# A fixed instruction order per period for an attention-and-mixer kernel: merged TensorE visits, a tail product inside another tile, and a last output tile in columns

## The chip, the cores and the metric

The kernel runs on one core of a Trainium2 chip. The metric is the device time of one execution in microseconds (us). A profile is one execution recorded by the hardware profiler; it gives every instruction of every engine with its start time. The engines are PE (TensorE, matrix products, with PEld for its weight loads), DVE (VectorE), ACT (ScalarE), POOL (GpSimd) and SP (SyncE, which here only issues transfers). PSUM is the small memory into which PE writes; SBUF is the large one from which all engines read.

## The reference, cut to what matters

Eight batches, each a Longformer attention followed by an MLP-Mixer block. Sequence 576, eight heads of 64, so a row of the block's input has 512 numbers.

```python
# attention, per batch and head; window 32, 8 global positions
mask   = (abs(i - j) <= 32) | is_global[i] | is_global[j]
attn   = softmax(where(mask, q @ k.T / 8, -1e9))
x      = concat_heads(attn @ v)                       # [576, 512]
# mixer, per batch
h      = relu(x.T @ w_tok1) @ w_tok2                  # token products: 576 -> 256 -> 576
u      = x + h.T
out    = u + relu(u @ w_ch1) @ w_ch2                  # channel products: 512 -> 1536 -> 512
```

576 rows are four tiles of 128 and one tail of 64. The tail has a path of its own in several places below.

## The kernel before: the parts that the change touches

The kernel works in periods. In period b the *dense* part is the channel products of batch b, and the *sparse* part, dealt out between the dense units, is attention and token products of batch b+1 and the scores of batch b+2. Every engine executes its instructions in the order in which they are written. Names of the steps as the text uses them:

- `T` transposes Q and K of two heads on PE, `TR` the last 64 rows; `TE`, `TRE` copy the results from PSUM to SBUF on DVE.
- `S_` the banded scores of two heads, in two parts, on PE in an arrangement of four 64x64 tiles; `SX` their exponential on ACT; `SM` the masks on DVE, first the 8 global columns (`eg`), then the band.
- `GK`, `OG` the global rows, on PE in 128x32 tiles; `LX`, `LM` and `RF` what ACT and DVE do with them.
- `PV` attention times V for one row tile, on PE in 128x64 tiles; then reciprocal and multiplication on DVE into `x16s`.
- `M1`, `M2` the two token products, 128x128; `M3` transposes u with DMA; `M4` the first channel product (4 matmuls of 512 columns and a ReLU on ACT), `M4l` the same for the tails of two batches; `M5` the second channel product (half a row tile: 6 matmuls of 512 columns).

```python
def S_(b, p, part):
    ps = pss([P, 2, 512], name=f"s{part}_{b}_{p}")          # one of two PSUM buffers, in turn
    for j in js:
        for par in range(2):
            nc.tensor.matmul(ps[o, par, i0 - a : i1 - a], lhsT=kT[r, HQ * j : HQ * j + HQ], rhs=qf[r, i0:i1], ...)
    st[b]["s", p, part] = ps
    if b > 0:
        SX(b, p, part)
# ... cut ...
def PV(b, tau):
    sh = 64 if tau == NT - 1 and b % 2 == 1 else 0
    tiles = ((2 * tau, 0), (2 * tau + 1, 64)) if tau < NT - 1 else ((2 * tau, sh),)   # last tile: one half only
    ps = (pss if b != 2 and tau % 2 else psv)([P, 2, 512], name=f"pv_{b}_{tau}")
    for hf in range(2):
        glob(hf)                      # 264 columns for each tile
        for hh in range(NP):
            local(hf, hh)             # 66 columns for each tile and head
    # ... cut: reciprocal and multiplication on DVE into x16s[b % 2][:, tau] ...
def M2(b, part):
    taus = ((0, 1), (2, 3), (4,))[part]
    ps = pss([P, 2, 512], name=f"hp_{b}_{part}")
    for i, tau in enumerate(taus):
        for ch in range(2):
            nc.tensor.matmul(ps[:, i, :], lhsT=w2[:, ch, P * tau - sh : P * tau - sh + P], rhs=s["a1"][:, ch, :], ...)
    # ... cut: x + ps on DVE; part 2 is the tail of 64 rows, 128x512 of which 64 rows are used ...
def M5(b, tau, part):
    if part == 0:
        s["o"] = psm([P, 512], name=f"op_{b}_{tau}")
    for j in range(6 * part, 6 * part + 6):
        nc.tensor.matmul(ps, lhsT=w, rhs=wc2[:, j, :], start=(j == 0), stop=(j == NJ - 1))
    # ... cut: part 1 adds u on DVE and stores 128 rows of 512 ...
# ... cut: the loads and the head (batch 0), which is written out step by step; its end: ...
    M2(0, 2)
    masks_a()
    for p in (None, 0):
        cast_qk(1, 0, p, V)           # casts of batch 1's q and k on DVE, after their loads
        cast_qk(1, 1, p, V)
# period 0: D is the next dense unit; n = 1, m = 2
u = [D, D, D, D, D, D, lambda: TR(n), lambda: globals_(n), D, lambda: t(n, 0), *c1[:2], D]
# ... cut ...
# second half of a later period, m = b + 2
return [D, s2(m, 0), D, lambda: t(m, 3), lambda: SM(m, 0), D, s2(m, 1), D, lambda: SM(m, 1), D, s2(m, 2), D,
        lambda: SM(m, 2), lambda: GK(m), lambda: v_odd(m), s2(m, 3), D, lambda: SM(m, 3), D, lambda: OG(m)]
```

`s2(m, p)` is both parts of the scores of one pair of heads; a later period has four such visits, three of `PV` (two tiles, two tiles, the last tile) and one of `TR`.

Of the kernel before, what the change touches and what calls it, by code (L numbers as in the profile page):

```python
# [8 lines left out]
F32 = mybir.dt.float32  # L9
# [16 lines left out]

def merge(sparse, dense):


    ts, td = sum(c for c, _ in sparse) or 1.0, sum(c for c, _ in dense) or 1.0  # L30
    i = j = 0
    a = d = 0.0
    while i < len(sparse) or j < len(dense):
        if j >= len(dense) or (i < len(sparse) and a / ts <= d / td):
            a += sparse[i][0]
            sparse[i][1]()
            i += 1
        else:
            d += dense[j][0]
            dense[j][1]()  # L40
            j += 1
# [3 lines left out]
def kernel(  # L45
# [27 lines left out]
    psS = ctx.enter_context(tc.tile_pool(name="psS", bufs=2, space=bass.MemoryType.PSUM))  # L73
# [5 lines left out]
    def pss(shape, dtype=F32, name="s"):  # L79
        return psS.tile(shape, dtype, tag="s", name=name)  # L80
# [4 lines left out]
    def psm(shape, dtype=F32, name="m"):  # L85
        return psM.tile(shape, dtype, tag="m", name=name)

# [156 lines left out]
    w1l = const.tile([P, 2, DTOK], F16)  # L244
# [7 lines left out]
    def load_w1l():  # L252
        nc.gpsimd.dma_start(out=w1l[0:LAST, 0], in_=moe_w_tok1[S - LAST : S, :])
        nc.gpsimd.dma_start(out=w1l[LAST:P, 1], in_=moe_w_tok1[S - LAST : S, :])
# [40 lines left out]
    def x_pads(i):  # L295
        nc.gpsimd.memset(x16s[i][LAST - 64 * i : P - 64 * i, NT - 1, :], 0.0)

# [35 lines left out]
    def gather_t(t):  # L333
        pg = (psm if t == 0 else psv)([P, 2, P], F16, name=f"pg_{t}")
        for ti in range(2):
            if t > 0:
                nc.vector.tensor_copy(out=g16[ti][t], in_=g32[ti][t])
            nc.tensor.transpose(out=pg[:, ti, :], in_=g16[ti][t], identity=ident)
        st[0]["gt", t] = pg
        if t > 0:  # L340
            GTE(t)
            GKE(t)
# [53 lines left out]
    def T(b, p):  # L396
        pT = (psm if b in (0, 2) else psv if b == 1 or p % 2 else pss)([P, 2, 512], F16, name=f"pT_{b}_{p}")
# [23 lines left out]
    def TR(b):  # L421
        pr = (psm if b in (0, 2) else psv)([P, 2, 4, NP * 16], name=f"pr_{b}")
# [8 lines left out]
        if b > 0:  # L431
            TRE(b)
# [10 lines left out]
    def S_(b, p, part):  # L443
        qf = qTs[b % 2][:, p].rearrange("p t x -> p (t x)")
        kT = kTs[b % 2][:, p]
        ps = pss([P, 2, 512], name=f"s{part}_{b}_{p}")
# [16 lines left out]
        if b > 0:  # L463
            SX(b, p, part)
# [43 lines left out]
    def GK(b):  # L508
        s = st[b]
        ps = (psv if b != 2 else pss)([P, 2, 512], name=f"gk_{b}")  # L510
# [8 lines left out]
        if b > 0:  # L519
            LX(b)  # L520
            LM(b)
# [12 lines left out]
    def OG(b):  # L534
        s = st[b]
        ps = (psv if b != 2 else pss)([P, 2, VW], name=f"og_{b}")
        for c in range(NT):
# [5 lines left out]
        rf = mb.tile([P, NP, 2, VW], F16, tag="rf", name=f"rf_{b}")  # L543
        nc.vector.tensor_tensor(
            out=rf, in0=ps.unsqueeze(1).to_broadcast([P, NP, 2, VW]),
            in1=blk.rearrange("p (n r) -> p n r", r=2).unsqueeze(3).to_broadcast([P, NP, 2, VW]), op=ALU.mult,
        )
        s["rf"] = rf
# [52 lines left out]
    def M1_0(p):  # L601
# [8 lines left out]
        for tt in range(2):  # L610
            for ch in range(NT):
                w = w1[:, ch, P * tt : P * tt + P] if ch < NT - 1 else w1l[:, 0, P * tt : P * tt + P]
                nc.tensor.matmul(ps[:, tt], lhsT=w, rhs=x16s[0][:, ch, cols], start=(ch == 0), stop=(ch == NT - 1))
# [33 lines left out]
    def PV(b, tau):  # L647
        s = st[b]

        sh = 64 if tau == NT - 1 and b % 2 == 1 else 0  # L650
        tiles = ((2 * tau, 0), (2 * tau + 1, 64)) if tau < NT - 1 else ((2 * tau, sh),)
        ps = (pss if b != 2 and tau % 2 else psv)([P, 2, 512], name=f"pv_{b}_{tau}")

        def glob(hf):
            for t, r0 in tiles:
                nc.tensor.matmul(  # L656
                    ps[r0 : r0 + 64, hf, 0 : NP * VW], lhsT=s["lf"][:, HQ * t : HQ * t + HQ],
                    rhs=s["rf"][:, 2 * hf : 2 * hf + 2], start=True, stop=False,
                )

        def local(hf, hh):
            h = NP * hf + hh
            for t, r0 in tiles:
# [7 lines left out]
        for hf in range(2):  # L671
            glob(hf)
            for hh in range(NP):
                local(hf, hh)
        r = slice(0, P) if tau < NT - 1 else slice(sh, sh + 64)
# [5 lines left out]
            in1=rr[r].unsqueeze(3).to_broadcast([P if tau < NT - 1 else 64, 2, NP, D]), op=ALU.mult,  # L681
        )

    def M1(b, ch):
        s = st[b]
        if ch == 0:
            ps = pss([P, 2, 512], name=f"a1p_{b}")
            s["a1p"], s["a1pp"] = [ps[:, 0], ps[:, 1]], ps
        ps = s["a1p"]
        for tt in range(2):  # L690
            w = w1[:, ch, P * tt : P * tt + P] if ch < NT - 1 else w1l[:, b % 2, P * tt : P * tt + P]
            nc.tensor.matmul(ps[tt], lhsT=w, rhs=x16s[b % 2][:, ch, :], start=(ch == 0), stop=(ch == NT - 1))  # L692
        if ch < NT - 1:
            return
# [13 lines left out]
    def M2(b, part):  # L708
        s = st[b]
        x16 = x16s[b % 2]  # L710
        taus = ((0, 1), (2, 3), (4,))[part]
        ps = pss([P, 2, 512], name=f"hp_{b}_{part}")
        sh = 64 if (part == 2 and b % 2) else 0
        for i, tau in enumerate(taus):
            for ch in range(2):
                nc.tensor.matmul(  # L716
                    ps[:, i, :], lhsT=w2[:, ch, P * tau - sh : P * tau - sh + P], rhs=s["a1"][:, ch, :],
                    start=(ch == 0), stop=(ch == 1),
                )
        if part < 2:  # L720
            nc.vector.tensor_add(out=s["u16"][:, 2 * part : 2 * part + 2], in0=x16[:, 2 * part : 2 * part + 2], in1=ps)  # L721
        else:
            r = slice(sh, sh + 64)
            nc.vector.tensor_add(out=s["ul"][r], in0=x16[r, NT - 1], in1=ps[r, 0])  # L724
# [13 lines left out]
    def M3p(b, part):  # L738
        s = st[b]
        if part == 0:  # L740
            s["uT"] = mb.tile([P, 4, 512], F16, tag="uT", name=f"uT_{b}")
            s["pu"] = psv([P, 4, 4, P], F16, name=f"pu_{b}")
        for tau in (2 * part, 2 * part + 1):
            for cc in range(4):
                nc.tensor.transpose(out=s["pu"][:, tau, cc, :], in_=s["u16"][:, tau, P * cc : P * cc + P], identity=ident)
        for tau in (2 * part, 2 * part + 1):
# [45 lines left out]
    def t(b, p):  # L792
# [285 lines left out]
```

## Time and profile before

| | before |
|---|---|
| device time, median of 3 | 336.51 us (335.84 to 337.73) |
| span of the profiled execution | 331.4 us |
| granted PE clock, mean | 1.000 |
| PE busy | 310.7 us, 3505 matmuls |
| DVE, ACT, POOL busy | 191.3, 155.4, 62.8 us |
| first channel unit of periods 0 to 7 starts at | 36.5, 79.1, 122.2, 158.7, 198.3, 232.5, 272.1, 300.3 us |
| last matmul starts at | 326.2 us |

How to read it: busy time is the union of an engine's instructions. A matmul's record runs from its start to the end of its pipeline, so matmuls overlap in the records (384 matmuls of the first channel product have a mean of 380 ns each and together 94.9 us), and an interval between two starts says more of PE's pace than a duration does. In the timeline `128*64` after the operation is the number of rows and columns of the array that the instruction uses, `x8` the number of instructions that were merged into the line, and the bracket at the end tells how long the engine stood idle before it and what ended the wait. The start times of the periods above are those of the first matmul of the tile `b1p` of each batch.

### The profile page before, as it was taken

To read this page: it belongs to the slowest core of one execution; us is meant where nothing else is said; L and a number is where in the kernel's file an instruction comes from. 1 tells how busy PE (TensorE), PEld (TensorE's weight loads), DVE (VectorE), ACT (ScalarE), POOL (GpSimd) and SP (SyncE) were. 2 spreads that over 40 slices of the span, in tenths; PEclk is the share of its full clock that TensorE was granted. 3 is DMA by queue.
4 is the path that set the end of the run, shared out by engine and by line. 5 is a ranking of instruction groups with operands and counts; after the bars stand their busy time and mean duration, and the time that the engine had idled before them with its cause. 6 is when DMAs were issued, how large, how long until landed. Compare 5 with 4: busy or idle time off the path is not lost.

```text
span 331.4 us, 8236 instructions
## 1 busy us (share of the span) xinstructions
PE 310.7 (94%) x3505; PEld 170.8 (52%) x3505; DVE 191.3 (58%) x414; ACT 155.4 (47%) x281; POOL 62.8 (19%) x95
## 2 busy tenths in 40 slices
PE   4898997997999999999999999999999999999994
PEld 4757544544455545454556445544556445444641
DVE  7388559769644876477737574577636574331021
ACT  3461676425765165725574336725673423504600
POOL 5796569500030004000310004000000000000000
PEclk9999999999999999999999999999999999999999
DMA  7899999994795929493499429693003111051012
GB/s 213 200 142 216 289 189 206 229 125 87 249 92 117 270 75 110 34 312 112 72 67 285 87 76 107 69 280 112 34 0 65 66 64 34 12 133 63 2 72 86
DMA packets 78198, 41.85 MB, mean 126 GB/s; under 512 B 54482, under 2 KB 72274, under 8 KB 78162
## 3 DMA queue, kind: packets, MB, share of 16 engines
q1 hardware_dynamic: 39552, 28.45, 32.4%
q0 software_dynamic: 38608, 12.88, 32.1%
q8 instruction: 27, 0.44, 0.6%
q14 instruction: 9, 0.07, 0.1%
q10 hardware_dynamic: 2, 0.00, 0.0%
HBM read 36.11 MB, written 9.44 MB: 137 GB/s over the span
## 4 chain that ended last, share of the span: by engine, by line
PE 67%; DVE 12%; DMA 11%; SPq 3%; issue 3%; ACT 1%; POOL 1%; DVEq 0%; POOLq 0%; ACTq 0%
PE op L781 25%; PE b1p L755 19%; DMA wc<-in_moe_w_ch_dram 8%; PE a1p L692 5%; PE hp L716 4%; PE pv L656 3%; PE b1lp L768 3%; PE pv L665 3%; PE pT L400 2%; PE s L458 2%; DVE e_all L481 2%; DMA lkr<-in_k_dram 2%; DVE vod L374 2%; DVE vod L373 1%; DVE osb L785 1%
## 5 line engine op out<-in xcount | busy, mean ns | idle before, releaser
L755 PE MATMUL b1p<-uT,wc 128*128 128x512 f16 x384 | 94.9, 380 | 0.8 <-ACT b L758 0.6
L758 ACT ACTIVATE b<-b1p 128x512 f16<-128x512 f32 x96 | 57.0, 598 | 76.6 <-PE b1p L755 76.2
L781 PE MATMUL op<-wc,b 128*128 128x512 f16 x384 | 90.0, 380 | 0.0
L470 ACT ACTIVATE e_all<-s 128x544 f16<-128x544 f32 (+1 forms) x64 | 40.9, 686 | 38.9 <-issue 26.0
L361 POOL DMA_DIRECT2D vsh<-in_v_dram x35 | 30.2, 866 | 133.6 <-DVE rr L678 118.1
L755 PEld LDWEIGHTS <-wc 128*128 128x128 f16 x384 | 34.9, 98 | 39.8 <-issue 2.2
L781 PEld LDWEIGHTS <-b 128*128 128x128 f16 x384 | 35.1, 98 | 39.0
L785 DVE TENSOR_TENSOR osb<-u,op 128x512 f32<-128x512 f16 x32 | 22.0, 686 | 53.1 <-PE op L781 51.0
L678 DVE RECIPROCAL rr<-pv 128x8 f32<-128x8 f32 (+1 forms) x35 | 7.1, 204 | 30.8 <-PE pv L665 30.8
L481 DVE TENSOR_TENSOR e_all<-e_all,bandm 128x616 f16<-128x616 f16 x56 | 24.3, 476 | 1.0
L679 DVE TENSOR_TENSOR x<-pv,rr 128x512 f16<-128x512 f32 (+1 forms) x35 | 24.2, 691 | 1.2
L406 DVE COPY qT<-pT 128x512 f16<-128x512 f16 x30 | 20.6, 686 | 7.2 <-PE pT L400 5.4
L721 DVE TENSOR_TENSOR u<-x,hp 128x1024 f16<-128x1024 f16 x14 | 17.0, 1218 | 12.1 <-PE hp L716 12.1
L412 DVE COPY kT<-pT 128x512 f16<-128x512 f16 x30 | 20.4, 682 | 1.6 <-PE pT L400 1.1
L716 PE MATMUL hp<-a,w 128*128 128x512 f16 x72 | 19.1, 379 | 1.3 <-DVE u L721 1.3
L656 PE MATMUL pv<-rf,lf 128*64 128x264 f16 x126 | 18.3, 283 | 0.9 <-DVE kgz L355 0.7
L386 ACT CAST kn<-lk 128x512 f16<-128x512 f32 x27 | 16.8, 622 | 3.1 <-DMA lk<-in_k_dram 3.1
L386 ACT CAST qn<-lq 128x512 f16<-128x512 f32 x27 | 16.5, 613 | 3.5 <-DMA lq<-in_q_dram 3.5
L458 PE MATMUL s<-qT,kT 64*64 64x136 f16 (+2 forms) x704 | 16.5, 217 | 1.8 <-DVE ul L724 0.7
L665 PE MATMUL pv<-vsh,e_all 128*64 128x66 f16 x280 | 18.0, 194 | 0.0
L665 PEld LDWEIGHTS <-e_all 128*64 128x64 f16 x504 | 17.9, 111 | 0.1
L458 PEld LDWEIGHTS <-kT 64*64 64x64 f16 x704 | 10.9, 107 | 13.3 <-issue 11.6
(175 smaller groups left out, 353.4 us busy)
## 6 DMA issues: line engine op xcount, KB each, us to landing
out_dram<-osb SPq DMA_DIRECT2D x32, 256.0 KB
lq<-in_q_dram SPq DMA_DIRECT2D x5, 1024.0 KB
lk<-in_k_dram SPq DMA_DIRECT2D x5, 1024.0 KB
wc<-in_moe_w_ch_dram POOLq DMA_DIRECT2D x6, 512.0 KB
vsh<-in_v_dram POOLq DMA_DIRECT2D x21, 128.0 KB
lq<-in_q_dram POOLq DMA_DIRECT2D x2, 1024.0 KB
lk<-in_k_dram POOLq DMA_DIRECT2D x2, 1024.0 KB
vsh<-in_v_dram POOLq DMA_DIRECT2D x14, 96.0 KB
```

What stands on the lines that cost most here:

```text
L361: nc.gpsimd.dma_start(out=vsh[b % 2][r0:r1, c, :, 0:D], in_=v[b, :, j0 : j0 + (r1 - r0), :].rearrange("h p d -> p h d"),)
L386: eng(out=(qn, kn)[ti][b % 2][:, :, hs].rearrange("p i h d -> p h i d"), in_=(lq, lk)[ti][:, hs])
L458: nc.tensor.matmul(ps[o, par, i0 - a : i1 - a], lhsT=kT[r, HQ * j : HQ * j + HQ], rhs=qf[r, i0:i1], start=b > 0, stop=b > 0 or j in js[-2:],)
L470: nc.scalar.activation(out=e2[:, :, a:z], in_=ps[:, :, 0 : z - a], func=AF.Exp, scale=scale)
L481: nc.vector.tensor_mul(out=e2[:, par], in0=e2[:, par], in1=bm)
L656: nc.tensor.matmul(ps[r0 : r0 + 64, hf, 0 : NP * VW], lhsT=s["lf"][:, HQ * t : HQ * t + HQ], rhs=s["rf"][:, 2 * hf : 2 * hf + 2], start=Tr ...
L665: nc.tensor.matmul(ps[r0 : r0 + 64, hf, VW * hh : VW * hh + VW], lhsT=e_all[:, h, lo : lo + HQ], rhs=(vod if t % 2 else vsh)[b % 2][:, tau ...
L716: nc.tensor.matmul(ps[:, i, :], lhsT=w2[:, ch, P * tau - sh : P * tau - sh + P], rhs=s["a1"][:, ch, :], start=(ch == 0), stop=(ch == 1),)
L755: nc.tensor.matmul(ps, lhsT=wc1[:, cc, P * j : P * j + P], rhs=s["uT"][:, cc, :], start=(cc == 0), stop=(cc == 3))
L758: nc.scalar.activation(out=s["b1"][:, j, :], in_=ps, func=AF.Relu)
L781: nc.tensor.matmul(ps, lhsT=w, rhs=wc2[:, j, :], start=(j == 0), stop=(j == NJ - 1))
L785: nc.vector.tensor_add(out=osb, in0=s["u16"][:, tau], in1=ps)
```

## The change

All instructions of a period are now written in one fixed list, in which each engine's part of a step has a word of its own (so `S` and its exponential `X` and its mask `M` can stand apart), and the PSUM buffer of each step is named in the list. With it:

- Visits of PE to the smaller tile arrangements are merged. In periods 2 to 5 the eight score parts come in 3 visits instead of 4, `PV` in 2 instead of 3 with `TR` inside the second, and `GK` and `OG` in one after another.
- The tail of the second token product (`M2` part 2) goes into the next batch's first `PV` tile: same arrangement (128x64), unused columns 264 to 391 of the same PSUM banks, 8 matmuls of 128 columns instead of 2 of 512. The addition (`AT`) becomes two operations of 64x256 on DVE.
- For that the last `PV` tile computes its 64 rows twice, the second time on partitions 64 to 127 with the two halves of the heads swapped, so that each x lies on the partition on which its part of the tail product comes out (20 matmuls instead of 10), and padding and a second copy of the last rows of `w_tok1` go away.
- The last output tile of the last batch is computed in three column pieces (256, 128, 128), each added and stored for itself, and it comes after the tail's tile.
- At the end of the head, the transposes of batch 1's first pair of heads and its `TR` now stand before the first dense unit of period 0; before, six dense units stood ahead of them.

The core of the diff:

```diff
+PLAN = [
+    """
+    nT.0.0 nR.v D D nr D nCQ.3 D D nGL nK.0 nCK.3 D nT.1.v nCK.2 nK.1 D nQ.0 nQ.1 D nCQ.2 mLP mLV D nS.0.1.1 nS.0.0.0
     ... cut: the rest of period 0, and period 1 ...
+    """
+    D nPV.0.v.h nNO.0 bAT nPV.1.1 nNO.1 nPV.2.0 nNO.2 mCQ mCK mCQ.0 D mCK.0 D D nA.0.1 nA.1.1 nA.2.1 mCQ.1 mCK.1 mR.m mr
+    nPV.3.v nNO.3 nPV.4.0 nNO.4 mCQ.2 mCK.2 D D nA.3.1 mT.0.v mQ.0 mK.0 mCQ.3 D nA.4.1 nRU mCK.3 mT.1.0 mQ.1 mK.1 mLV
+    mGL oLQ D D nH.0.1 nAD.0 nU.0 D nH.1.0 nAD.1 nU.1 mT.2.v mQ.2 mK.2 D mT.3.1 mQ.3 mK.3 D D mS.0.0.1 mX.0.0 mS.0.1.0
+    mX.0.1 mS.1.0.v mX.1.0 D mM.0 D mS.1.1.0 mX.1.1 mS.2.0.1 mX.2.0 mS.2.1.v mX.2.1 D mM.1 D mM.2 mS.3.0.0 mX.3.0
+    mS.3.1.1 mX.3.1 mVO mM.3 D D mGK.v mLX mLM mOG.0 mRF D
+    """,
     ... cut: the same with M4l units, for odd periods ...
+    def HT(b, hf, ps, last=False):
+        s = st[b]
+        s["ht"] = ps
+        for ch in range(2):
+            for half in range(2):
+                c0 = 256 * half + P * hf
+                nc.tensor.matmul(
+                    ps[64 * half : 64 * half + 64, hf, NP * VW : NP * VW + P], lhsT=w2[:, ch, S - LAST : S],
+                    rhs=s["a1"][:, ch, c0 : c0 + P], start=last and ch == 0, stop=last and ch == 1,
+                )
+    def M5c(b, tau, lo, hi):
+        for j in range(NJ):
+            nc.tensor.matmul(
+                ps[:, 0 : hi - lo], lhsT=s["b1"][:, j, P * tau : P * tau + P], rhs=wc2[:, j, lo:hi], ...
+            )
+        nc.vector.tensor_add(out=osb[:, 0 : hi - lo], in0=s["u16"][:, tau, lo:hi], in1=ps[:, 0 : hi - lo])
+        nc.sync.dma_start(out=out[b, P * tau : P * tau + P, lo:hi], in_=osb[:, 0 : hi - lo])
     def dense(b):
-        u += [(1.3, lambda t=t, i=i: M5(b, t, i)) for t in range(4 + b % 2) for i in range(2)]
+        if b < B - 1:
+            u += [(1.3, lambda t=t, i=i: M5(b, t, i)) for t in range(4 + b % 2) for i in range(2)]
+        else:
+            u += [(1.3, lambda t=t, i=i: M5(b, t, i)) for t in (0, 1, 2, 4) for i in range(2)]
+            u += [(0.0, lambda lo=lo, hi=hi: M5c(b, 3, lo, hi)) for lo, hi in ((0, 256), (256, 384), (384, 512))]
```

A word is a step with the batch ahead of it (b, n = b+1, m = b+2, o = b+3) and its arguments after it; the last argument of `S`, `T`, `PV`, `H` (M2), `A` (M1), `GK` and `OG` is the PSUM buffer (0, 1, v or m), `D` is the next dense unit, `Q` and `K` are the two copies after `T`, `NO` what follows `PV` on DVE.

## The prediction

> **What bounds the kernel now.** I read the page first.
>
> ```profile
> span 331.4 us, 8236 instructions
> PE 310.7 (94%) x3505; PEld 170.8 (52%) x3505; DVE 191.3 (58%) x414; ACT 155.4 (47%) x281; POOL 62.8 (19%) x95
> ```
>
> PE is the bound: from 80 us on it is idle for hardly 2% of the time. But a record runs to the end of the pipeline, so "busy" hides both a slow pace and short drains. The next view is the timeline of PE around a visit to the small tile arrangement (start, duration, operation).
>
> ```profile
> 201.32 1.90 PE L755 MATMUL b1p<-uT,wc 128*128 128x512 f16 x8
> 203.15 0.30 PE L656 MATMUL pv<-rf,lf 128*64 128x264 f16 x2
> ...
> 204.11 0.19 PE L665 MATMUL pv<-vsh,e_all 128*64 128x66 f16 x1
> 204.24 1.04 PE L755 MATMUL b1p<-uT,wc 128*128 128x512 f16 x4
> ```
>
> Eight matmuls of 512 columns at a pace of 216 ns end at 203.05, yet the first 128x64 matmul starts at 203.15; the last one starts at 204.11, and the next 128x128 one 0.13 later instead of 0.03. Over all pairs of neighbours in the trace: 512 columns to 512 columns 216 ns (316 pairs in b1p), 512 columns to the first matmul of another arrangement 309 ns (19 pairs to pv, 15 to s), and back 125 to 126 ns where a further matmul of the visit would have come after some 28. So a switch costs about 0.093 on the way in and 0.097 on the way out: **0.095 us each**, idle time that PE's busy share doesn't show.
>
> Third, the list of what PE waited for (total, times, longest):
>
> ```profile
> PE og L539 <- DVE eg L476: 2.2, 3, 1.3
> PE hp L716 <- DVE u L721: 1.3, 4, 0.3
> PE s L458 <- DVE ul L724: 0.7, 1, 0.7
> PE s L458 <- ACT e_all L470: 0.6, 1, 0.6
> PE pT L400 <- DVE kT L412: 0.6, 1, 0.6
> ```
>
> The first two come back in every period: the global rows wait for the last mask, and the tail product M2 part 2 waits for a PSUM buffer that DVE still reads.
>
> Fourth, the end of the head on PE and on DVE, because the change puts the first transposes of batch 1 ahead of the first dense unit:
>
> ```profile
> 36.07 0.59 PE L716 MATMUL hp<-a,w 128*128 128x512 f16 x2
> 36.50 5.38 PE L755 MATMUL b1p<-uT,wc 128*128 128x512 f16 x24
> 41.81 0.32 PE L427 MATMUL pr<-ident,qr 128*64 128x64 f16 x8
> ```
>
> ```profile
> 38.02 0.41 DVE L386 CAST qn<-lq 128x512 f16<-128x512 f32 x1
> 40.57 0.43 DVE L386 CAST kn<-lk 128x512 f16<-128x512 f32 x1 [2.14 <-DMA lk<-in_k_dram]
> ```
>
> The cast that these transposes need starts at 40.57, when its load has landed. Before, six dense units cover that wait.
>
> **What the Trainium skill says.** "TensorEngine Tiling (Array Packing)", section Key Properties: changing the tiling mode drains TensorE. The trace agrees and sizes it: 0.095 us. "TensorE: Matmul & The Clock Gate", section Back-to-back issue gap: N/2.4 + 2.5 ns, so 216 at 512 columns and 56 at 128; the trace has 216 and 56. The same page, section What's actually happening: the clock falls to half after an idle window of some 3.4 us; no stretch of this trace shows it after the start. "DMA: Bandwidth & Descriptors", section Anatomy of one DMA: a fixed part of about 2 us, most of it the receipt from the target, that doesn't shrink with the size. Here the last add ends at 327.26 and the span at 331.4, 4.1 us with two issues of 1.12 in sum, which doesn't contradict it.
>
> **The working.** I took the mean start-to-start interval of every kind of neighbouring pair in the trace of before (waits over 60 ns left out) and added them up in each program's own order: PE's time if it waits for nobody. For before this gives, by period, 37.1, 41.1, 34.0, 38.6, 33.4, 38.6, 28.2, 25.9, together 276.9 us; the starts of the periods give 42.6, 43.1, 36.5, 39.6, 34.2, 39.6, 28.2, 25.8, together 289.7. The difference, 12.7, is waits: 5.5, 2.0, 2.5, 1.0, 0.8, 1.0, 0, 0. (Period 4 as a test: 33.35 and the waits that I find one by one, 0.79, make 34.14 of the 34.17 measured.)
>
> *Switches.* Counted in the two programs: 25, 32, 21, 19, 19, 19, 6, 0 before, 141; 21, 22, 12, 12, 12, 12, 4, 0 after, 95. 46 x 0.095 = **-4.4**.
>
> *Tail product.* Seven times 2 matmuls of 512 columns go: 7 x 2 x 0.216 = **-3.0**. Six times 8 matmuls of 128 columns come, two beside each other on the two column halves; an estimate of half of 56 ns each gives 6 x 8 x 0.028 = +1.3. For the last batch the 8 have a visit of their own at 56 ns: +0.45. Together **+1.8**. The ten matmuls that the doubled last PV tile adds run beside the ten that were there: a one-sided tile takes 0.50 (207.36 to 207.96, less a switch) and a two-sided one 0.49. They cost nothing.
>
> *Columns at the end.* 12 x 0.109 + 24 x 0.056 = 2.65 for 12 x 0.216 = 2.59: **+0.1**.
>
> Sum -5.5; the added-up intervals of the new order give 35.8, 40.2, 32.4, 37.7, 32.4, 37.7, 27.8, 26.5, and 0.95 that moved into the head: 271.6, or **-5.3**, and I take that.
>
> *Waits, steady periods.* I walked periods 2 and 3 of the new list by hand with effective durations of before (mask step 1.0, its global part 0.18; two V copies 1.36; output add 0.60; T copy 0.60; u add 1.2; exponentials 0.6 and 0.74). The hardest place is OG, which needs the global columns of the last mask. From the end of the second half of output tile 1: DVE 0.20 + 0.60 add, 1.0 mask 1, 1.0 mask 2, 1.36 copies, 0.18, semaphore 0.05 = 4.4 us. PE meanwhile: 1.30 output, 0.09 switch, 0.39 scores, 2 x 1.30 output, 0.09, 0.28 GK = 4.74. OG finds it ready; 0.33 of wait goes (0.92 in period 2's OG). The scores after the channel part need the buffer of the fourth T: from the start of the unit ahead of M2, DVE is done with the last copy at 7.4, PE there at 7.5. Tight, no wait. The wait of M2 part 2 (0.25) has gone with it. I leave 0.25 a period for what I missed: 1.0 in place of 5.3 in periods 2 to 5, and 0.2 in the last two.
>
> *Waits, period 0 and 1.* In period 0, PE now reaches the transposes of batch 1 at about 36.5, but the cast of k ends at 41.0: **+4.5 us of waiting**, with nothing in the change that brings that load earlier but 32 KB less of weights. Behind it things ease: the first channel unit starts at some 41.7. The two waits of about 0.77 go, OG's 1.55 shrinks, as more stands between, and the transposes of u no longer meet a buffer that isn't free; I put the rest at 1.5, so 6.0 instead of 5.5. Period 1: OG behind two channel units only, about 0.4, and its start behind DVE's copies, 0.6: 1.0 instead of 2.0.
>
> Waits after: 6.0 + 1.0 + 1.0 + 0.2 = 8.2 instead of 12.7: **-4.5**.
>
> *The end.*
>
> ```profile
> 326.57 0.69 DVE L788 TENSOR_TENSOR osb<-ul,op 128x512 f32<-128x512 f16 x1 [1.90 <-PE op L781]
> 327.29 1.12 SPq L790 DMA_DIRECT2D out_dram<-osb  x2
> ```
>
> The last matmul is 128 columns instead of 512 (-0.16), the last add a quarter as wide (0.69 to about 0.25, an estimate from its width), and one transfer is issued instead of two (1.12 to about 0.5): **-1.2**.
>
> Sum: -5.3 - 4.5 - 1.2 = -11.0. I give back 1.0 for a wait that I overlooked and for the clock, and predict 336.5 - 10.0 = **326.5 us**.
>
> **Rivals.** *The wait at 36.5 is hidden or far worse.* If the load of k lands earlier in the new order, the 4.5 us don't come: 322. Against it: POOL's queue of loads is the same up to there, and the 10 us stretches from 20 to 50 show the DMA engines saturated (shares 1.05, 1.09, 1.61). If on the other hand the idle PE loses its clock there, some 3.4 us at half speed cost up to 2 or 3 us more: 329. For it: 4.4 of the next 4.6 us are idle; against it: four transposes of q break the stretch near 38.5, so that an idle window fits in only by chance.
>
> *DVE takes over the bound.* It is 58% busy, but in the second half of a period the mask, the V copies and the output adds stand close together, and merging takes away the dense units that used to give DVE time between visits. If DVE comes 1 us late at OG and again at the scores, in four periods, 5 to 8 us of the gain go: 331 to 334. The measured steps say 4.4 against 4.74 and 7.4 against 7.5, so the margin is there but thin.
>
> *ACT becomes the wait:* three score parts in a visit queue 2 us of exponentials, but the output units behind need no ACT, and channel units with two buffers only meet casts (0.6). I give it 0.2 a period at most.
>
> **Range and chances.** 321.5 is all of it without the wait at the start; 331.5 has DVE late in half of the places. Faster by over 2% means under 329.8, 3.3 above my number, so 0.82; within 2% 0.16; slower would need two of the rivals at once, 0.02.
>
> **What would show it.** The first b1p matmul at about 41.7 instead of 36.5, with PE waiting for the cast of kn; starts of periods 2 to 5 apart by 32.5 to 33 and 38 us; og no longer waiting for eg in these and no hp wait at all; PE's busy time lower by some 8; the end 4 us behind the last matmul. Wrong it would be if periods 2 to 5 kept their lengths though the switches fall from 19 to 12 (the switch would then not be the cost), or if PE waited in them for the copies of T or for eg.

## The result, and the profile after

| | before | after |
|---|---|---|
| device time, median of 4 (range) | 336.17 us (334.35 to 337.73) | 324.59 us (323.22 to 324.90) |
| span of the profiled execution | 331.4 us | 322.8 us |
| PE busy | 310.7 us | 307.4 us |
| first channel unit of periods 0 to 7 starts at | 36.5, 79.1, 122.2, 158.7, 198.3, 232.5, 272.1, 300.3 | 44.5, 83.7, 124.4, 156.7, 194.3, 226.6, 264.2, 291.9 |
| lengths of periods 0 to 6 | 42.6, 43.1, 36.5, 39.6, 34.2, 39.6, 28.2 | 39.1, 40.8, 32.3, 37.6, 32.3, 37.6, 27.7 |
| from period 7's start to the last matmul's start, and on to the end | 25.9, 5.3 | 26.4, 4.5 |

Ratio 0.965, 95% interval 0.9593 to 0.9706. Predicted were 326.5 us (321.5 to 331.5); the time lies inside the range, 1.9 us under the number. The sum came out, but two of its parts did not: the start of period 1 comes 4.6 us later than before instead of at the same time, and periods 1 to 6 save 12.95 us instead of 10.9.

The page after, its first line, its busy times and the row of the granted clock (one digit for each fortieth of the span, 8.07 us):

```profile
span 322.8 us, 8501 instructions
...
PE 307.4 (95%) x3641; PEld 176.5 (55%) x3641; DVE 192.0 (59%) x423; ACT 155.1 (48%) x281; POOL 61.9 (19%) x93
...
PEclk9997679999999999999999999999999999999999
```

PE's busy time fell by 3.3 us only, where the prediction had 8. The row of the clock says why: slices 4 to 6, about 24 to 48 us, ran at 0.7 and 0.6 of full speed on average. There the first matmuls of the channel product start 427 ns apart instead of 216, so PE is busy longer for the same work.

What PE waited for (total, times, longest), with lines of the start-up left out:

```profile
PE pT L423 <- DVE qn L409: 2.2, 1, 2.2
...
PE pv L598 <- issue: 1.1, 1, 1.1
PE og L555 <- DVE eg L495: 0.9, 2, 0.7
PE s L479 <- DVE kT L435: 0.6, 1, 0.6
...
PE pT L423 <- DVE kn L409: 0.4, 1, 0.4
```

`hp` is gone from the list. The two `og` waits that are left lie in periods 0 and 1; periods 2 to 5 have none. New is `pT` waiting for the casts of batch 1, more for that of q (`qn`, 2.2 us) than for that of k (`kn`, 0.4). In the timeline of PE (start, duration, operation, and in the bracket the idle time with what ended it):

```profile
40.24 0.59 PE L741 MATMUL hp<-a,w 128*128 128x512 f16 x2
43.08 0.40 PE L423 MATMUL pT<-ident,qn 128*128 128x128 f16 x4 [2.24 <-DVE qn L409]
43.83 0.40 PE L423 MATMUL pT<-ident,kn 128*128 128x128 f16 x4 [0.35 <-DVE kn L409]
...
44.53 1.80 PE L816 MATMUL b1p<-uT,wc 128*128 128x512 f16 x5
```

The first `b1p` matmuls start 0.226, 0.215, 0.299 us apart, and the next seven intervals are 0.426 or 0.427, twice the usual 0.216: the clock falls some 0.6 us into the dense unit. The stretches of the same place (length; PE busy, instructions; granted clock; DMA share; GB/s) show two separate slow stretches, one ahead of the wait and one behind it:

```profile
28.00:32.00 4.00, 4.00 (x57) 0.50 1.22 234
32.00:36.00 4.00, 4.00 (x57) 0.50 1.06 319
36.00:40.00 4.00, 3.73 (x44) 0.72 1.05 284
40.00:44.00 4.00, 1.39 (x13) 1.00 1.24 207
44.00:48.00 4.00, 4.00 (x30) 0.64 1.63 187
48.00:52.00 4.00, 4.00 (x25) 0.94 1.67 134
```

The first, from 28 to 38 us, lies in the head, which the change doesn't touch. The profiles of e1, e6 and e10 have it as well (e10 is the kernel before with one move), the profile of before doesn't, and in after the last matmuls of the head start 4.2 us later than in before (40.24 and 36.07). So the two spans are not quite alike: they lie 8.6 us apart, the medians 11.6. The second stretch follows the new wait. Whether it belongs to the change is the first question to the experiments.

A steady period in one line (PE, PEld, DVE, ACT and POOL busy, clock, DMA), period 4 before and after:

```profile
198.33:232.50 34.17, 33.73 (x375) 17.33 (x374) 21.28 (x43) 18.07 (x33) 4.20 (x5) 1.00 0.75 138
```

```profile
194.33:226.61 32.28, 32.28 (x392) 17.25 (x391) 21.68 (x45) 18.22 (x33) 4.19 (x5) 1.00 0.69 134
```

PE is busy for 32.28 of 32.28 us: no wait is left. DVE has more to do than before and holds nothing up.

The end, on DVE:

```profile
317.29 0.42 DVE L861 TENSOR_TENSOR osc<-u,oc 128x256 f32<-128x256 f16 x1 [0.62 <-PE oc L857]
317.95 0.29 DVE L861 TENSOR_TENSOR osc<-u,oc 128x128 f32<-128x128 f16 x1 [0.25 <-PE oc L857]
319.84 0.29 DVE L861 TENSOR_TENSOR osc<-u,oc 128x128 f32<-128x128 f16 x1 [1.60 <-DMA out_dram<-osb]
```

The last add waits 1.60 us, and not for its matmuls, but for an earlier store to give one of three output buffers back.

### The profile page after: what moved, and what is told of

Its sections match the earlier page's. It is cut to its first block, busy times and chain, and to the rows that moved or that the text cites. A ratio compares the mean times of both kernels' runs of the same rounds, so it can differ in the third digit from the quotient of the medians.

```text
span 322.8 us, 8501 instructions
## 1 busy us (share of the span) xinstructions
PE 307.4 (95%) x3641; PEld 176.5 (55%) x3641; DVE 192.0 (59%) x423; ACT 155.1 (48%) x281; POOL 61.9 (19%) x93
## 4 chain that ended last, share of the span: by engine, by line
PE 85%; DVE 7%; ACT 3%; DMA 2%; issue 1%; SPq 0%; DVEq 0%; ACTq 0%
PE op L842 27%; PE b1p L816 24%; PE a1p L718 5%; PE hp L741 4%; PE pT L423 4%; PE b1lp L829 3%; PE pv L675 3%; PE pv L684 3%; PE s L479 3%; PE warm L236 2%; DMA lq<-in_q_dram 2%; ACT e_all L489 2%; PE a1p L632 1%; DVE e_all L500 1%; PE pr L450 1%
## 5 line engine op out<-in xcount | busy, mean ns | idle before, releaser
L816 PE MATMUL b1p<-uT,wc 128*128 128x512 f16 x384 | 93.4, 385 | 0.0
L842 PE MATMUL op<-wc,b 128*128 128x512 f16 x372 | 85.8, 380 | 0.0
L816 PEld LDWEIGHTS <-wc 128*128 128x128 f16 x384 | 35.6, 99 | 38.9 <-issue 2.6
L842 PEld LDWEIGHTS <-b 128*128 128x128 f16 x372 | 34.3, 98 | 39.1
L489 ACT ACTIVATE e_all<-s 128x544 f16<-128x544 f32 (+1 forms) x64 | 40.1, 685 | 23.6 <-PE s L479 18.0
L846 DVE TENSOR_TENSOR osb<-u,op 128x512 f32<-128x512 f16 x31 | 21.2, 685 | 41.4 <-PE op L842 41.4
L705 DVE TENSOR_TENSOR x<-pv,rr 128x512 f16<-128x512 f32 x35 | 24.2, 692 | 1.2
L479 PE MATMUL s<-qT,kT 64*64 64x136 f16 (+2 forms) x704 | 15.2, 215 | 0.6 <-DVE kT L435 0.6
L423 PE MATMUL pT<-ident,qn 128*128 128x128 f16 x128 | 12.9, 225 | 2.2 <-DVE qn L409 2.2
L741 PE MATMUL hp<-a,w 128*128 128x512 f16 x58 | 14.8, 379 | 0.0
```

Source lines behind the costliest of these rows:

```text
L423: nc.tensor.transpose(out=pT[:, ti, P * i : P * i + P], in_=n[b % 2][:, i, 2 * p : 2 * p + 2, :], identity=ident)
L489: nc.scalar.activation(out=e2[:, :, a:z], in_=ps[:, :, 0 : z - a], func=AF.Exp, scale=scale)
L741: nc.tensor.matmul(ps[:, i, :], lhsT=w2[:, ch, P * tau : P * tau + P], rhs=s["a1"][:, ch, :], start=(ch == 0), stop=(ch == 1),)
L816: nc.tensor.matmul(ps, lhsT=wc1[:, cc, P * j : P * j + P], rhs=s["uT"][:, cc, :], start=(cc == 0), stop=(cc == 3))
```

## The experiments

My theory: the gain comes from fewer switches and fewer waits in periods 1 to 6; the transposes at the start of period 0 take some of it back, by their wait and by the clock that PE loses behind it. Rivals: the slow clock belongs to the head and would be there anyway; the merges save waits, not switches; the tail product is what pays. All medians in us (range, number of executions), each with its ratio to the kernel before and the 95% interval:

| | median | ratio |
|---|---|---|
| after | 324.59 (323.22 to 324.90, 4) | 0.965 [0.9593, 0.9706] |
| e1_late_t | 320.11 (317.25 to 322.37, 4) | 0.9509 [0.9414, 0.9604] |
| e7_late_t2 | 318.83 (318.07 to 321.83, 6) | 0.9538 [0.9484, 0.9593] |
| e11_ob5 | 318.55 (317.07 to 320.86, 6) | 0.9523 [0.948, 0.9566] |
| e8_casts_dve | 319.86 (317.84 to 321.59, 6) | 0.9535 [0.9484, 0.9586] |
| e9_head_filler | 320.77 (319.11 to 324.34, 6) | 0.9548 [0.9497, 0.96] |
| e6_filler_both | 321.76 (320.80 to 324.24, 6) | 0.9591 [0.9532, 0.965] |
| e2_filler | 323.00 (321.68 to 323.67, 4) | 0.9613 [0.9534, 0.9693] |
| e5_no_columns | 324.09 (323.70 to 324.61, 4) | 0.9653 [0.9577, 0.9728] |
| e4_tail_apart | 327.04 (326.40 to 327.56, 4) | 0.9761 [0.97, 0.9821] |
| e3_unmerged | 328.18 (324.52 to 328.31, 4) | 0.9744 [0.9648, 0.984] |
| e10_before_early_t | 342.06 (340.56 to 343.14, 4) | 1.0183 [1.0119, 1.0248] |

The intervals of e3, e4 and e10 reach across 2%, so against the kernel before these three stay unclear at that mark; each is read against the kernel from which it was made. By the mean clock, three of after's four executions have the head's slow stretch (0.976 and 0.977; the fourth, 323.22 us, has 0.987) but only two of e7's six, so a difference of medians holds a part of the head, and where it counts executions with the stretch are set against such, and those without against those without.

### The transposes at the start of period 0

**e1_late_t** puts the first transposes of batch 1 behind five dense units again, all else as after:

```diff
-    nT.0.0 nR.v D D nr D nCQ.3 D D nGL nK.0 nCK.3 D nT.1.v nCK.2 nK.1 D nQ.0 nQ.1 D nCQ.2 mLP mLV D nS.0.1.1 nS.0.0.0
+    D D D D D nT.0.0 nR.v nr D nGL nCQ.3 nK.0 nCK.3 nT.1.v nCK.2 nK.1 D nQ.0 nQ.1 D nCQ.2 mLP mLV D nS.0.1.1 nS.0.0.0
```

> The changed kernel, but with the transposes of batch 1's first heads and of its last rows behind five dense units again. Theory A (PE waits 2.9 us for the cast of q and k at the end of the head, and the idle stretch then costs half the clock from 45.2 to 48.6, another 1.7 us): both go, so about 4 us less than the changed kernel, 320 to 321 us, no slow clock right behind the first b1p. Theory B (the load of k is the bound there wherever its readers stand, the wait only moves): within 0.7 us of the changed kernel, 324 to 325 us. The slower clock between 28 and 38 us lies before this place and should stay in both.

The median is 4.5 us under that of after, a part of it from the heads. In its profile the dense units start 0.43 us behind the head's last matmul (41.48, then 41.91); period 0 keeps its length (39.28 instead of 39.12), and at 49 us a new wait of 0.85 appears: the second pair's transposes wait for a DVE copy. So the early transposes do cost, and the move can be done better.

**e7_late_t2** takes six units instead of five and pulls the copies forward, so that no PSUM buffer is waited for:

```diff
+    D D D D D D nT.0.0 nR.v nr nGL D nK.0 nQ.0 nCQ.3 nCK.3 nT.1.v nCK.2 D nK.1 nQ.1 D nCQ.2 mLP mLV nS.0.1.1 nS.0.0.0
```

> The changed kernel with the transposes of batch 1's first heads and its TR behind six dense units, and the next transposes one unit later than in the run before that moved them, so that these don't wait for the copies of TR. Theory A: neither the wait at the end of the head nor the one of 1.0 us at the next transposes is left, no slow clock behind the first b1p; 3 to 5 us less than the changed kernel, 316.5 us where the head keeps its clock and 320.5 where it doesn't; the median 318 to 320. Theory B (DVE's copies come later and make the scores of period 0 wait instead): the same as with five units, 320 us in the median.

318.83 us, 5.8 under after. Like with like it is less: with the head's slow stretch 321.13 and 321.83 against 324.53 to 324.90, without it 318.07 to 319.03 against 323.22, so 3 to 5 us. Its stretches at the end of the head:

```profile
36.00:40.00 4.00, 4.00 (x22) 1.00 1.03 299
40.00:44.00 4.00, 4.00 (x43) 1.00 1.24 210
44.00:48.00 4.00, 3.98 (x48) 1.00 1.45 195
```

PE is hardly idle and has its full clock. The timeline of PE shows the work in place of the wait:

```profile
36.09 0.59 PE L741 MATMUL hp<-a,w 128*128 128x512 f16 x2
36.52 5.39 PE L816 MATMUL b1p<-uT,wc 128*128 128x512 f16 x24
41.74 0.39 PE L423 MATMUL pT<-ident,qn 128*128 128x128 f16 x4
```

24 dense matmuls stand between, and the casts are done when PE gets to the transposes. Period 1 starts at 77.10, 2.0 us before that of the kernel before, 6.55 before that of after; 4.2 of the latter are the head's own late start, which this profile doesn't have. PE busy is 301.8 us, 8.9 under before.

**e10_before_early_t** does the same move alone in the *old* kernel: the first transposes and `TR` ahead of the first dense unit (and another PSUM buffer for these transposes), nothing else of the change:

```diff
-        u = [D, D, D, D, D, D, lambda: TR(n), lambda: globals_(n), D, lambda: t(n, 0), *c1[:2], D]
+        u = [lambda: T(n, 0), lambda: TR(n), D, D, D, D, D, D, lambda: globals_(n), lambda: TE(n, 0), D, *c1[:2], D]
```

> The kernel before with one part of the change alone: the transposes of batch 1's first heads and its TR ahead of the first dense unit of period 0. Theory A (PE waits 4.5 us there for the cast of k and then runs some 3.4 us at half the clock): the first b1p at 41.7 us or later instead of 36.5, two to four us longer in all, 338 to 340 us, no run with a mean clock over 0.992. Theory B (period 0 waits for loads and ACT later anyway, 5.5 us of it, and these waits take up the delay): within 1 us of before, 335 to 336.5 us.

342.06, 6.8 us over the kernel before as measured beside it (335.29), and more than the 2 to 4 that were expected. Without the head's slow stretch it is 340.56 and 341.29 against 334.20 to 334.64. The wait is there, and behind it the first two `b1p` matmuls take 1.03 us, where two take 0.59 at full clock:

```profile
45.05 0.40 PE L400 MATMUL pT<-ident,qn 128*128 128x128 f16 x4 [3.01 <-DVE qn L386]
...
46.20 1.03 PE L755 MATMUL b1p<-uT,wc 128*128 128x512 f16 x2
```

The cost of the early transposes is thus shown from both sides: in like executions 3 to 5 us taken out of the new kernel, 6 to 7 put into the old one.

### Wait or clock?

**e2_filler** fills the first part of the wait with matmuls whose result is not used; **e6_filler_both** fills both parts (42 behind the head's last matmul, 30 between the transposes of q and of k). Nothing else is changed.

```diff
     M2(0, 2)
+    W(40, True)     # e2; W(42, True) in e6
     AD(0, 2)
...
+            if (b, p, ti) == (1, 0, 0):
+                W(30, True)     # e6 only
```

> The changed kernel with 40 idle products of 128 columns (2.2 us, their result is not used) put into the wait before the transposes of batch 1. Theory A (the slow clock behind the wait comes from PE's idleness there): the wait itself stays, period 0 begins at the same time, and its first eight to sixteen b1p matmuls run at 216 ns instead of 427, so 1.5 to 2 us less: 322.5 to 323 us. Theory B (the slow clock comes from something else, such as the load on the chip in the head): no difference, 324 to 325 us.

> The changed kernel with 42 idle products of 128 columns before the first transposes of batch 1 and 30 more between those of q and those of k (their results are not used), so that PE works in both of its waits there. Theory A (idleness in these waits makes PE lose half its clock behind them): no slow clock behind the wait, the first b1p matmuls at 216 ns and period 0 at about 37.2 us instead of 39.1; 322 us where the head itself keeps its clock. Theory B (the clock falls there for another reason): period 0 stays at 39.1 us.

e2 still has a wait, and one slow stretch behind it:

```profile
35.72 2.40 PE L236 MATMUL warm<-ident 128*128 128x128 f16 x40
38.23 0.40 PE L423 MATMUL pT<-ident,qn 128*128 128x128 f16 x4
41.52 0.40 PE L423 MATMUL pT<-ident,kn 128*128 128x128 f16 x4 [2.89 <-DVE kn L409]
```

```profile
40.00:44.00 4.00, 2.48 (x25) 0.80 1.24 207
44.00:48.00 4.00, 4.00 (x15) 0.78 1.71 185
```

Period 0 has 39.12 us, as in after: against the expectation, filling the first part alone did not bring the clock back, and the median of 323.00 is about that of after's one execution without the head's slow stretch. In e6 (two slow slices in the head, as in after) the wait is full of work, and the clock stays:

```profile
40.00:44.00 4.00, 3.92 (x65) 1.00 1.23 209
44.00:48.00 4.00, 4.00 (x52) 1.00 1.60 190
48.00:52.00 4.00, 4.00 (x26) 1.00 1.67 122
```

Period 0 takes 37.48 us with the same waits as in after (0.7 at `og`, 0.6 at `s`): **the lost clock alone is 1.6 us**, although PE does no useful work earlier (the first dense unit starts at 45.66, 1.1 later than in after, behind the fillers). So of the 1.6 only 0.5 is left at the start of period 1. The median is 2.8 us under after, but like with like the difference is 0.5 (324.14 and 324.24 with the head's slow stretch) and 1.4 to 2.4 (320.80 to 321.81 without). So the rival that the second slow stretch comes from the head falls: the head of e6 is as slow, and the stretch is gone.

The e2 profile, whose head runs at full clock, also shows the wait at its true size: the head's last matmul starts at 35.29, the first dense unit at 42.22. There the cast of k is held by its load:

```profile
41.03 0.43 DVE L409 CAST kn<-lk 128x512 f16<-128x512 f32 x1 [2.86 <-DMA lk<-in_k_dram]
```

In after the head is 4.2 us late, so the load has landed meanwhile, and the gap is 4.29 us instead of 6.9. What PE waits for there is DVE itself, which after the head's last product has the tail's sum, the band mask and two casts to do before it comes to `qn`:

```profile
40.87 0.68 DVE L754 TENSOR_TENSOR ul<-x,hp 64x512 f16<-64x512 f16 x1 [1.02 <-PE hp L741]
42.20 0.82 DVE L409 CAST qn<-lq 128x512 f16<-128x512 f32 x1
```

So a late head costs after less (1.3 to 1.7 us by its executions) than it costs e7, which doesn't wait (2.1 to 3.8).

### Switches

**e3_unmerged** splits the merged visits of periods 2 to 6 again, in the otherwise unchanged order (20 switches instead of 12 in a steady period, 34 more in all; four score visits, `PV` in three, `GK` and `OG` apart):

```diff
-    ... nNO.1 nPV.2.0 ...  mr nPV.3.v nNO.3 nPV.4.0 nNO.4 mCQ.2 mCK.2 D D nA.3.1
+    ... nNO.1 D nPV.2.0 ... mr D nPV.3.v nNO.3 nPV.4.0 nNO.4 mCQ.2 mCK.2 D nA.3.1
-    mS.0.0.1 mX.0.0 mS.0.1.0 mX.0.1 mS.1.0.v mX.1.0 D mM.0 D mS.1.1.0 mX.1.1 mS.2.0.1 mX.2.0 mS.2.1.v mX.2.1 D mM.1
-    D mM.2 mS.3.0.0 mX.3.0 mS.3.1.1 mX.3.1 mVO mM.3 D D mGK.v mLX mLM mOG.0 mRF D
+    mS.0.0.1 mX.0.0 mS.0.1.0 mX.0.1 D mM.0 mS.1.0.v mX.1.0 mS.1.1.1 mX.1.1 D mM.1 D mS.2.0.0 mX.2.0 mS.2.1.v mX.2.1
+    D mM.2 mS.3.0.1 mX.3.0 mS.3.1.0 mX.3.1 mVO mM.3 D mGK.v mLX D mLM mOG.0 mRF D
```

> The changed kernel with the merged visits taken apart in periods 2 to 6 (four visits of scores, PV in three, the 64-row product and the global rows on their own): 20 changes of arrangement a period instead of 12, same matmuls, 34 more changes in all. Theory A (each change costs 0.095 us): periods 2 to 5 are each 0.76 us longer (33.0 and 38.4 us) without any wait of PE, 3.2 us in all: 327.8 us. Theory B (the steady periods became shorter because waits went, and the changes of arrangement are free): periods stay at 32.3 and 37.6 us, 324.6 us.

Period 4 of this kernel:

```profile
195.78:228.95 33.17, 33.17 (x391) 17.15 (x390) 22.40 (x45) 18.22 (x33) 4.20 (x5) 1.00 0.82 134
```

The same matmuls, the full clock, PE busy without a gap in both, and 0.90 us more than after. Periods 2 to 5 together are 3.45 us longer for 32 switches: **0.108 us for each**, of which 0.093 on the way in and 0.098 on the way out are seen between starts, and the rest is in slower first pairs of a visit (some 0.03 a visit, that is, per two switches). The way into one visit of e3 in the timeline:

```profile
215.82 1.24 PE L834 MATMUL op<-wc,b 128*128 128x512 f16 x5
216.99 0.46 PE L471 MATMUL s<-qT,kT 64*64 64x72 f16 x22
```

Five `op` matmuls from 215.82 at 0.216 start the last one at 216.68; the next start is 0.31 later. The rival that merging only saves waits falls: here nothing waits, and the time is longer all the same. The median is 3.6 us above that of after; one of the four executions took only 324.52, so the profile carries this reading.

### The tail product

**e4_tail_apart** takes the tail product out of the `PV` tile and gives it back its own two matmuls of 512 columns and its own buffer:

```diff
-    D nPV.0.v.h nNO.0 bAT nPV.1.1 ...  mQ.2 mK.2 D mT.3.1 mQ.3 mK.3
+    D nPV.0.v   nNO.0     nPV.1.1 ...  mQ.2 mK.2 D nH.2.m mT.3.1 nAD.2 nU.2 mQ.3 mK.3
```

> The changed kernel with the tail of the second token product on its own again (two matmuls of 512 columns behind part 1, its sum on DVE there), no HT in the first PV tile and none for the last batch; visits stay merged. Theory A (the tail inside PV saves matmul time alone: 0.43 us for 0.25 a period, and the last batch pays 0.44): period 0 0.4 us longer, periods 1 to 6 about 0.2 us longer each (32.5 and 37.8 us), period 7 0.4 us shorter, 1 us in all. Theory B (what counted was the wait of that product for its PSUM buffer): the wait comes back, another 0.25 us in each of periods 2 to 6, so these are 0.4 to 0.5 us longer each and the whole 2 to 2.5 us.

327.04, 2.5 us over after. Period 4:

```profile
194.84:227.74 32.90, 32.66 (x385) 17.15 (x384) 21.70 (x45) 18.22 (x33) 4.20 (x5) 1.00 0.70 135
```

32.90 instead of 32.28. The separate product brings a wait at its new place: the next unit's PSUM buffer is held until DVE has added the tail.

```profile
213.56 1.03 PE L804 MATMUL b1p<-uT,wc 128*128 128x512 f16 x4
214.83 1.47 PE L830 MATMUL op<-wc,b 128*128 128x512 f16 x6 [0.24 <-DVE ul L740]
```

The idle time in the record is 0.24; from start to start the wait costs 0.40, since the last of the four matmuls starts at 214.21 and the next would have followed at 214.43. The rest of the 0.62, some 0.2, is PE's own time: the 8 narrow matmuls lengthen the first `PV` visit from 1.58 in e4 to 1.80 in after, so they cost 0.22, where the two wide ones cost 0.43. Period 0, at 40.84, has a further wait of 1.7 us for a copy of k. In the last period the order turns: e4 is 0.37 us shorter there, since after gives the last tail a visit of its own. The tail product pays twice as much by the wait that it takes away as by the work. It was one term among several, not what made the change pay.

### The end

**e5_no_columns** computes the last tile whole, in the old order:

```diff
-        if b < B - 1:
+        if b < B:
```

> The changed kernel with the last batch's output tiles in the old order and whole, the tail's tile last. Theory A (add, transfer issue and last matmul behind PE's end are shorter with pieces): 0.8 to 1.2 us longer, 325.4 to 325.8 us, and 5.3 us from the last matmul's start to the end instead of 4.4. Theory B (the receipt of the last transfer sets the end whatever its size): within 0.3 us, 324.3 to 324.9 us.

The median is 0.5 us under after, with ranges that overlap and the same ratio: the times don't tell the two apart. Against after's one execution without the head's slow stretch (323.22) e5 is 0.5 to 1.4 longer. The profiles say: from the last matmul's start to the end 5.25 us instead of 4.47, and period 7 up to that start 26.22 instead of 26.44, so the columns bring some 0.6. Not in every execution: in the profile of e2, which has the columns, the end takes 5.29. Why not more is in the last add of after, shown above: it waits 1.60 us for an output buffer, in e2 2.41.

**e11_ob5** is e7_late_t2 with five output buffers instead of three:

```diff
-    ob = ctx.enter_context(tc.tile_pool(name="ob", bufs=3))
+    ob = ctx.enter_context(tc.tile_pool(name="ob", bufs=5))
```

> The kernel e7_late_t2 with five output buffers in place of three, nothing else. My theory is that the last column add on VectorE waits 1.6 us for a store to give an output buffer back, so that the columns bring only part of what they could: with five buffers that wait is gone, the time from the start of the last matmul run to the end of the span goes from about 4.5 us to about 3.3 us, and the median is about 1.1 us under that of e7_late_t2 (318.8), near 317.7 us. The rival theory is that the three stores of the last tile, issued one behind the other by SyncE, set the end: then the wait moves from VectorE to the queue, the end stays at 4.2 us or more, and the time does not change by more than the spread.

The last add comes when its matmuls are done, and the queue needs 1.51 us for the three issues that took 2.56 with the wait in between:

```profile
312.09 0.29 DVE L861 TENSOR_TENSOR osc<-u,oc 128x128 f32<-128x128 f16 x1 [0.38 <-PE oc L857]
```

The end is 3.43 us behind the start of the last matmul instead of 4.46. That part is as the theory has it, and the rival, the queue, doesn't hold the end. In the medians the gain is 0.3, not 1.1, with ranges of nearly 4 us in both, since three of the six executions here have a slow clock (0.983 and 0.984) and two of e7's. Like with like the gain is there: 317.07 to 317.55 against 318.07 to 319.03, and 319.56 to 320.86 against 321.13 and 321.83. So the fastest kernel of the study is this one, by about 1 us.

### Two tries that brought nothing

**e8_casts_dve** moves two casts of batch 1 from ACT to DVE in e7, because in e7's period 0 the scores wait 1.28 us for ACT's exponentials; **e9_head_filler** adds 14 unused matmuls in the head of e7, against the slow stretch there.

```diff
-    for p in (None, 0):
+    for p in (None, 0, 3):        # e8, and the words nCQ.3 nCK.3 go from the list
...
     RF0(3)
+    W(14, True)                   # e9
```

> The kernel with the late transposes (six dense units first) in which two of batch 1's casts go from ACT to DVE, at the end of the head where DVE waits for the load. Theory A (what PE waits for in period 0 now, 1.45 us at the scores of the third pair, is ACT, which has the ReLUs, the exponentials and four casts in a row there): 1.2 us of ACT go, PE's wait shrinks to some 0.3 us, the median falls by 0.7 to 1.2 us to about 318 us. Theory B (that wait is PSUM's turn and comes back elsewhere, at OG or at the first token product): the same 318.8 us.

> The kernel with the late transposes and 14 idle products of 128 columns (0.8 us, result not used) in the head before the first token product of batch 0, where PE stood idle for 0.75 us. Theory A (the slow clock from 28 to 38 us, which a part of all runs of every kernel has, comes from PE's idle stretches just before): no run under a mean clock of 0.99, all runs at 318 to 319 us, spread under 1 us. Theory B (it comes from a stall of some other kind and not from this gap): again about a third of the runs at 321 to 322 us with a clock of 0.98, the rest up to 0.8 us longer.

e8: 319.86 us; period 0 becomes 0.64 shorter, but its start comes 0.79 later, so that period 1 starts at 77.25 instead of 77.10. No gain, and the shorter period is not to be put down to the casts: e11, with the casts where e7 has them, shows the same (0.61 shorter after a start 0.63 later, period 1 at 77.11). e9: 320.77 us, and its profile, the slowest of its six executions, still has a clock of 0.57 from 28 to 32 us. No gain either. But this profile shows the clock fall once more, in period 1, where PE waits 2.02 us for the transposed tail of u; from 100 to 104 us the granted clock is 0.60:

```profile
99.29 1.41 PE L829 MATMUL b1lp<-uTl,wc 128*128 128x128 f16 x16 [2.02 <-DMA uTl<-ul]
```

What starts the slow stretch of the head stays open: profiles with it (after, e1, e6, e9, e10) all show PE idle for 0.9 to 1.5 us in the middle of a `PV` tile of the head, waiting for nothing that the profile names; but e8 and e3 show 0.9 and 0.7 at that place and don't have it, and my fillers stood ahead of that place, not in it.

## Why the prediction was right, and where it was wrong

**Switches: mechanism right, size a little low.** 46 at 0.095 gave -4.4. The traces have 42 fewer: the count of 95 left out the two switches of the last tail's own visit and the two that moved into the head. At the 0.108 of e3 that is 4.5 (an estimate for periods 0 and 1, which e3 leaves alone). What a visit costs inside itself was missed. (The eight added-up periods and the 0.95 make 271.45, not 271.6; nothing hangs on it.)

**Tail product: right.** The 8 narrow matmuls were put at 0.22 and take 0.22; the doubled last `PV` tile costs nothing that can be seen. That the wait for its buffer goes as well was predicted and is what e4 brings back.

**Waits in the steady periods: right in kind, too careful in size.** "I leave 0.25 a period for what I missed": nothing was missed. The list of waits was misread in one point: in before `og` waits for the mask in periods 0 to 2 and `hp` for its buffer in periods 2 to 5, so neither comes back in every period. Periods 2 to 5 were to take 141.2 us with that and take 139.8; period 1 was to take 41.2 and takes 40.8. This term makes the 2 us by which periods 1 to 6 beat the number: PE's own time was put at 208.2 us for them, and 208.3 in all is what they take.

**DVE as the new bound: the rival fell, by less than I thought.** I had 4.4 us against 4.74 at `OG`. In period 3 of after the last mask's global part runs on DVE as `OG` comes up on PE:

```profile
188.50 0.18 DVE L495 TENSOR_TENSOR eg<-e_all,egm 128x80 f16<-128x80 f16 x1
```

```profile
188.65 0.22 PE L555 MATMUL og<-vsh,eg 128*32 128x132 f16 x1
188.65 0.19 PE L536 MATMUL gk<-qT,kgz 128*32 128x64 f16 x1
188.66 0.55 PE L555 MATMUL og<-vsh,eg 128*32 128x132 f16 x19
```

The mask ends at 188.68, while the first `og` starts at 188.65 (its record begins within the mask's tail, so the two meet to within the precision of the records). The margin of 0.34 was in truth next to none; that one more operation on DVE there would be a wait is likely, but no run shows it.

**The start of period 0: the step that failed.** I wrote that PE waits 4.5 us, that the first dense unit starts at some 41.7 "with nothing in the change that brings that load earlier", and gave the loss of the clock to a rival that "fits in only by chance", because four transposes of q would break the stretch. Three things were wrong. First the size: in profiles with a head on time (e2, e3, e4, e5) the first dense unit starts at 42.1 to 43.7, 0.4 to 2.0 us later than I had it. Second, what is waited for: not the load of k alone. In these four profiles PE first waits for `qn`, mostly behind DVE's other work (1.9 to 2.3 us in e3, e4 and e5; e2 fills that part), and then for `kn` (1.9 to 3.0), and in after it is nearly all DVE. Third, the transposes don't protect the clock. It fell at the wait in after, e2, e3, e4, e5 and e10 alike: behind 2.2 and 0.4 us split by the transposes in after, 2.9 in e2, 3.0 in e10; e6, which fills both parts, keeps it, and then period 0 takes 37.48, for which my working had 37.3. The loss is 1.6 us for one stretch, less than the "up to 2 or 3 us more" of the rival. The Trainium skill ("TensorE: Matmul & The Clock Gate", section What's actually happening) speaks of an idle window of some 3.4 us; the shortest slow stretches here have that length, but a gap of 2.9 us, in after one of 2.2 followed by 0.4, and in e9's period 1 one of 2.02 was enough to bring one on, so by the measurement shorter gaps are not safe. Waits of 1.73 and 1.75 us (e4 and e10, later in period 0) brought none. With all this, the start of period 1 comes at 81.3 to 83.1 in those profiles, at 83.65 in after, instead of 79.0.

**The end: mis-sized.** The -1.2 was worked out from the last matmul, add and transfer alone, and left out that the pieces need more output buffers at a time. It is -0.8 in the profiles of before and after, and -1.8 with five buffers.

**What would have shown it.** "PE's busy time lower by some 8" came out as 3.3, since slow matmuls are busy longer; e7 without slow stretches has 8.9. "Starts of periods 2 to 5 apart by 32.5 to 33 and 38": 32.28 and 37.62. `og` and `hp` as predicted. So the nearness of the number is in part luck: a start of period 1 that was 2 to 4 us worse where the head is on time (81.3 to 83.1) was met by periods 1 to 6 that were better by 2 and by the 1.0 given back. The other part of the luck is that a late head costs after only 1.3 to 1.7 us, while before takes 338.15 and 338.27 at a mean clock of 0.983 and 333.82 and 333.99 at 1.000, which lowers the median of after against that of before. Without the early transposes, which brought none of the gain, it would have been about 16 us (e7: 335.3 before to 318.8).

## What to carry to other kernels

Count the arrangement changes of TensorE and price them from the trace: at 0.1 us each, merging visits paid 3.7 us in periods 2 to 6 alone (e3), in a kernel whose PE looked 94% busy. Before work is moved to the front of a phase, ask when its *data* lands and what the engine that prepares it has to do first, and cover a wait with useful matmuls rather than let TensorE idle: here every wait of 2.0 us or more from the end of the head on was paid for a second time in the clock. When a last tile is cut into pieces, give each piece a buffer.

## What of the hardware I had not expected

- The slow stretches come in multiples of one length. The clock lost in the 4 us windows (one minus the granted share, times 4, summed) is 1.7 us behind the wait in after, e2 and e10 and in period 1 of e9, 3.4 at the wait in e3, e4 and e5, and 5.1 in the heads of after, e1, e6 and e10: at half clock that is 3.4, 6.8 and 10.2 us, one, two or three times the same stretch. Inside it the `b1p` matmuls start 427 ns apart instead of 216.
- A two-sided `PV` tile costs what a one-sided one costs, 0.49 us against 0.50, and the 8 matmuls of 128 columns on two column halves cost 0.22 us: two beside each other take what one takes alone (0.056).
- A store holds its output buffer for 2 us or more after its issue. In after the buffer that the last add waits for was filled by the tail's add; the queue issued that tile's transfers from 316.69 to 317.82, and the buffer was free at 319.84, 2.0 us after the last issue. In e7 it is 2.0 as well (311.25 to 313.26), in e2 2.8 (315.63 to 318.46).
